# Sigmoid attention and a silu layer: the last two batches' first product by Strassen, after all attention

## The chip, the cores and the metric

The kernel runs on one core of a Trainium2 chip, as one launch. The metric is the device time of the launch in microseconds; the profile is of one execution, and its times are counted from that execution's first instruction. The engines are TensorE (PE, matrix products into PSUM), VectorE (DVE), ScalarE (ACT, activations and copies), GpSimd (POOL) and SyncE (SP, here only an issuer of transfers). Each engine works through its own queue in order; semaphores tie the queues together.

## The reference

```
q, k, v: 8 batches x 12 heads x 448 x 64 (float32);  w_in: 768 x 2048;  w_out: 2048 x 768
scores = q @ k.T / 8 - log(448)
x      = sigmoid(scores) @ v            # heads joined: 3584 rows x 768
h      = x @ w_in                       # 3584 x 2048
g      = h * sigmoid(h)                 # silu
out    = g @ w_out                      # 3584 x 768
```

## The kernel before, in words

All operands are float16 on the chip. **Attention.** Heads are taken in 24 groups of four (three groups a batch, two pairs each), and the 448 keys of a group in 7 chunks of 64, `NCH`; one (group, chunk) is a *tile*. `scores` (line 182) makes a tile with four 64x64 matmuls of 448 columns into PSUM `psc`, and ACT turns it into `attnT` by a sigmoid. `values` (line 218) multiplies the seven tiles of a group by v in 28 matmuls into `pav`, and DVE writes the result, times 64 (`SX`), to `xT[b]`, two of its six slices of 128 rows by 448. A batch is *ready* when its three groups are done. k and q are cast, put into rows (`kr`, `qr`) and transposed by transfers on SP's queue, four groups ahead (`dma_transpose`).

**h.** `h_unit(b, fc)` (line 255) makes one of 16 slices of 128 columns of h for batch b, transposed: six accumulating matmuls of 448 columns into `ph`. ACT takes the sigmoid (`tsig`) and DVE multiplies `ph` by it into `gTr`, which holds 16 slices for a pair of batches (896 columns).

**out.** `out_set` (line 319) makes 256 rows of the output by Strassen's scheme: seven products of 8 matmuls of 384 columns over blocks of `gTr` (sums `S1` to `S4` of them, made by DVE at the set's start) and of w_out (sums `T1` to `T4`, made once), with ACT copying the first product to `m1` and DVE adding up the rest (`plus`) into `osb`. Its first product reads slices 0 to 7 of the first block, its second slices 8 to 15. A pair of batches has 7 blocks of 128 rows: three sets, and the seventh blocks of two pairs (one of them put aside in `kept` by ACT) share a fourth.

**Order.** The kernel writes the order out itself; nothing is rescheduled. h and out are one generator, `all_moe` (line 421), that yields after each matmul. Attention runs in bursts of two or three tiles (`burst`, line 586), and after each burst `stretch` (line 449) pulls matmuls from the generator until a pace in nanoseconds is used up, with other weights for h (0.72) and for sets (1.28):

```
paces = {1: 1600, 2: 2400, 3: 2500, 4: 3400, 5: 3200, 6: 3000, 7: 2800}
        ns = paces[n // NT_B]
        tiles = burst(n, TILES[n // NT_B])
        n += tiles
        stretch(ns * tiles / 2)
```

What is left of the generator when attention ends runs alone. In the last pair that is: h of batch 6, its first set while batch 7's attention still runs, then h of batch 7, two sets and the shared set. PSUM is split into two double banks (`pssc`, for scores) and four single ones (`ps1`, for everything else), SBUF into tagged pools that are reused in turn.

Of the kernel before, what the change touches and what calls it, by code (L numbers as in the profile page):

```python
# [17 lines left out]
def kernel(  # L18
# [9 lines left out]
    nc = tc.nc  # L28
# [116 lines left out]
    def pe_transpose(g, pieces=(("k", 0, 4), ("k", 4, NCH), ("q", 0, 4), ("q", 4, NCH))):  # L145
        if ("k", g) not in qkT:
            new_qkT(g)
        for name, c0, c1, *copy in pieces:
# [12 lines left out]
                dst[:, c0 * P : c1 * P], ptr[:, : (c1 - c0) * P]  # L161
            )

    def dma_transpose(g, name, copy):
        if ("k", g) not in qkT:
            new_qkT(g)
        rows = p3.tile([P, NCH, 2, D], F16, tag=f"{name}r", name=f"{name}r")
        copy(rows, flat[name, g].rearrange("p j c d -> p c j d"))  # L168
        nc.sync.dma_start_transpose(
            out=qkT[name, g], in_=rows.rearrange("p c j d -> p (c j d)")  # L170
        )

    attnT = {}

    late = []

# [5 lines left out]
    def scores(g, ch, banks=None, put_off=False):  # L182


        attnT[g, ch] = p12.tile([P, 2, S], F16, tag="attnT", name="attnT")
        if banks is None:
            psc = ps_sc.tile([P, 2, 512], F32, tag="pssc", name="psc")
            banks = [psc[:, j] for j in range(2)]
            parts = [(attnT[g, ch], psc[:, :, :S])]
        else:  # L190
            parts = [(attnT[g, ch][:, j], banks[j][:, :S]) for j in range(2)]
        for half in range(2):
            own = slice(half * HP, (half + 1) * HP)
            for j in range(2):
                rows = slice(j * D, (j + 1) * D)
                nc.tensor.matmul(  # L196
                    banks[j][own, :S],
                    qkT["k", g][rows, ch, own],
                    qkT["q", g][rows, :, own],
                    start=True,  # L200
                    stop=True,
                )
        if put_off:
            late.extend(parts)
            return
        for to, psc in parts:
            nc.scalar.activation(to, psc, AF.Sigmoid, bias=bias_s, scale=QKSCALE)  # L207
# [10 lines left out]
    def values(g, end=NCH):  # L218
        b, iq = divmod(g, NQ)
        if b not in xT:  # L220
            assert b < 2 or b - 2 in h_done
            xT[b] = p2.tile([P, NPAIR, S], F16, tag="xT", name="xT")
        pav, done_rounds = part_of.pop(g, None) or (
            [ps_1.tile([P, 512], F32, tag="ps1", name="pav") for _ in range(2)],
            0,
        )
        for ch in range(done_rounds, end):
            at = attnT.pop((g, ch))
            for half in range(2):
                own = slice(half * HP, (half + 1) * HP)  # L230
                for j in range(2):
                    nc.tensor.matmul(  # L232
                        pav[half][j * D : (j + 1) * D, :S],
                        flat["v", g][own, j, ch, :],
                        at[own, j, :],
                        start=(ch == 0),
                        stop=(ch == NCH - 1),
                    )
        if end < NCH:
            part_of[g] = pav, end  # L240
            return
        for half in range(2):
            nc.vector.tensor_scalar_mul(xT[b][:, half * NQ + iq, :], pav[half][:, :S], SX)  # L243
        if iq == NQ - 1:
            ready.add(b)

# [69 lines left out]
    def row_blocks(m, g):  # L316
        return [rows_of[2 * m + u // NCH, u % NCH] for u in (2 * g, 2 * g + 1)]

    def out_set(a1, rows1, a2, rows2, last=False):
        nonlocal hold, weight  # L320
        weight = SET_WEIGHT
        lo, hi = slice(0, NHC), slice(NHC, NFC)
        osb = [p4.tile([P, DMODEL], F32, tag="osb", name="osb") for _ in range(2)]
        c11, c12 = (osb[0][:, nh * NO2 : (nh + 1) * NO2] for nh in range(2))
        c21, c22 = (osb[1][:, nh * NO2 : (nh + 1) * NO2] for nh in range(2))
        m1 = p2.tile([P, NO2], F32, tag="m1", name="m1")
        sg = [cpool.tile([P, NHC, P], F16, tag=f"S{i}", name=f"S{i}") for i in range(1, 5)]

        def store(rows, o, cols, engines):
            for at, (row, eng) in enumerate(zip(rows, engines)):  # L330
                eng.dma_start(row[:, cols], o[at * HP : (at + 1) * HP, cols])

        left, right, whole = slice(0, NO2), slice(NO2, DMODEL), slice(0, DMODEL)

        def product(a, w):
            po = ps_1.tile([P, 512], F32, tag="ps1", name="po")
            for fc in range(NHC):
                nc.tensor.matmul(  # L338
                    po[:, :NO2], a[:, fc, :], w[:, fc, :], start=(fc == 0), stop=(fc == NHC - 1)
                )  # L340
                if fc < NHC - 1:
                    yield 163
            return po[:, :NO2]

        def plus(o, po, x, sign=ISX):
            nc.vector.scalar_tensor_tensor(  # L346
                out=o, in0=po, scalar=sign, in1=x, op0=ALU.mult, op1=ALU.add
            )

        nc.vector.tensor_sub(sg[2], a1[:, lo], a2[:, lo])  # L350
        nc.vector.tensor_add(sg[0], a2[:, lo], a2[:, hi])
        po = yield from product(a1[:, lo], wq[0][0])
        nc.scalar.activation(m1, po, AF.Copy, scale=ISX)  # L353
        late_sigmoid()
        nc.vector.tensor_sub(sg[1], sg[0], a1[:, lo])
        hold = False
        yield 163
        po = yield from product(a1[:, hi], wq[1][0])
        plus(c11, po, m1)
        nc.vector.tensor_sub(sg[3], a1[:, hi], sg[1])  # L360
        if last:
            store(rows1, osb[0], left, (nc.sync, nc.sync))
        yield 163
        po = yield from product(sg[2], tw[3])
        plus(c22, po, m1)
        yield 163
        po = yield from product(sg[1], tw[2])
        plus(c22, po, c22)
        plus(c12, po, m1)
        yield 163  # L370
        po = yield from product(a2[:, hi], tw[4])
        plus(c21, po, c22, -ISX)
        yield 163
        po = yield from product(sg[0], tw[1])
        plus(c22, po, c22)
        plus(c12, po, c12)
        store(rows2, osb[1], whole, (nc.sync, nc.sync))
        yield 163
        po = yield from product(sg[3], wq[1][1])
        plus(c12, po, c12)  # L380
        if last:
            store(rows1, osb[0], right, (nc.sync, nc.scalar))
        else:
            store(rows1, osb[0], whole, (nc.sync, nc.sync))
        yield 163


    by_h1 = {3: 6, 6: 7, 9: 8}
    early = [h_unit(0, fc) for fc in range(2)]
    sums = w_sums()  # L390

    def moe_h(b):
        for fc in range(NFC):
            yield from early[fc] if b == 0 and fc < 2 else h_unit(b, fc)
            if b == 1:
                if fc >= 2:
                    next(sums)
                if fc in by_h1:
                    for name in ("k", "q"):
                        dma_transpose(by_h1[fc], name, act_copy)  # L400
                    if by_h1[fc] == 8:

                        nc.gpsimd.tensor_copy(gate, qkT["q", 8][:1, 0, :1])
                        for to in (10, 11, 12):
                            load("kq", to)

    def moe_set(m, g):
        step = out_set(block(g), row_blocks(m, g), block(g + 1), row_blocks(m, g + 1))
        for i, ns in enumerate(step):
            if m % 2 == 0 and g == 2 and i % 8 == 4 and i < 32:  # L410
                fcs = slice(i // 8 * 4, i // 8 * 4 + 4)
                nc.scalar.activation(kept[:, fcs], block(NCH - 1)[:, fcs], AF.Copy)
            if m == 0 and g == 0 and i in (10, 14):
                next(sums)
            if m == 0 and g == 0 and i in (24, 40):
                dma_transpose(9, "k" if i == 24 else "q", nc.vector.tensor_copy)
                if i == 40:
                    load("kq", 13)
            yield ns

    def all_moe():
        for m in range(B // 2):
            yield from moe_h(2 * m)
            if m > 0:
                yield from moe_set(m, 0)
            yield from moe_h(2 * m + 1)
            if m == 0:
                yield from moe_set(m, 0)
            yield from moe_set(m, 2)
            yield from moe_set(m, 4)  # L430
            if m % 2 == 1:
                g = NCH - 1
                yield from out_set(
                    kept, row_blocks(m - 1, g), block(g), row_blocks(m, g), m == B // 2 - 1
                )

    later = []
# [144 lines left out]
            do(*what)  # L582

    TILES = {2: 3, 3: 2, 4: 3, 5: 3, 6: 3, 7: 3}
    paces = {1: 1600, 2: 2400, 3: 2500, 4: 3400, 5: 3200, 6: 3000, 7: 2800}
    def burst(n, tiles):

        new = units[n : n + (tiles if not waiting else 2)]
# [56 lines left out]
```

## Time and profile before

| | |
|---|---|
| median of 3 runs | 378.19 us (377.76 to 378.33) |
| the profiled execution | 377.84 us, span 376.0 us |
| granted TensorE clock | 1.000 |
| busy: PE, DVE, ACT, POOL | 367.9, 233.9, 243.2, 66.1 us |
| h matmuls (128x448) | 768 |
| output matmuls (128x384) | 784 |

A line of a group reads: line of the kernel, engine, operation, what is written and from what, shapes, count, then busy microseconds and mean nanoseconds of one, then the idle time of that engine just before them and who ended it. Busy PE is modelled from pipelined matmuls, so the spacing of matmuls in the chain of waits is the better price of one: the last 96 of h and the last 168 of out stand there as one piece each. Start to start, operations of one engine come closer than their means say, since the end of one overlaps the next.

### The profile page before, as it was taken

How to read it: one execution, taken by the hardware profiler on the slowest of the kernel's cores; microseconds unless marked ns; L12 is line 12 of the kernel's file. 1: busy time of each engine (PE TensorE's matmuls, PEld its weight loads, DVE VectorE, ACT ScalarE, POOL GpSimd, SP SyncE). 2: the span in 40 equal slices, each digit the busy share in tenths (PEclk: the TensorE clock that was granted, in tenths of full speed). 3: DMA queues.
4: the chain of work that ended last, by engine and by line, in shares of the span. 5: the costliest groups of instructions: out<-in, count | busy, mean ns of one | idle time of the engine just before them, and what ended most of it. 6: DMA issues, size and time to landing. Idle time of an engine off the chain costs nothing.

```text
span 376.0 us, 7623 instructions
## 1 busy us (share of the span) xinstructions
PE 367.9 (98%) x3081; PEld 189.2 (50%) x3081; DVE 233.9 (62%) x417; ACT 243.2 (65%) x355; POOL 66.1 (18%) x99
## 2 busy tenths in 40 slices
PE   7999999999999999999999999999999999999995
PEld 3554445555554455455555545544555445555663
DVE  2664447997666466548676547645675457556773
ACT  5998886778766866676557676677866685243000
POOL 8566432053211002102120200000010000000000
PEclk9999999999999999999999999999999999999999
DMA  8999999959999909909499834546072300200333
GB/s 131 200 204 201 205 203 204 180 89 142 215 178 182 217 2 111 189 32 118 71 160 161 145 92 75 51 108 75 0 149 36 85 2 2 54 30 2 83 86 84
DMA packets 65698, 42.79 MB, mean 114 GB/s; under 512 B 36096, under 2 KB 62208, under 8 KB 65664
## 3 DMA queue, kind: packets, MB, share of 16 engines
q0 software_dynamic: 27072, 22.58, 42.5%
q1 hardware_dynamic: 38240, 19.44, 29.0%
q8 instruction: 24, 0.39, 0.4%
q10 hardware_dynamic: 352, 0.30, 0.2%
q14 instruction: 10, 0.08, 0.1%
HBM read 45.61 MB, written 11.01 MB: 151 GB/s over the span
## 4 chain that ended last, share of the span: by engine, by line
PE 91%; DMA 3%; ACT 2%; POOL 2%; issue 1%; DVE 0%; POOLq 0%; ACTq 0%
PE ph L262 38%; PE po L338 34%; PE psc L196 9%; PE pav L232 8%; DMA qf<-in_q_dram 3%; ACT attnT L207 1%; POOL kf L82 1%; POOL vf L82 1%; PE ptrq L153 0%; POOL qf L82 0%; ACT tsig L274 0%; DVE gTr L276 0%; ACT attnT L180 0%; PE ptrk L153 0%; DVE osb L346 0%
## 5 line engine op out<-in xcount | busy, mean ns | idle before, releaser
L207 ACT ACTIVATE attnT<-psc,bias_s 128x896 f16<-128x896 f32 (+1 forms) x168 | 138.5, 894 | 45.1 <-PE psc L196 44.9
L262 PE MATMUL ph<-xT,w_in_sb 128*128 128x448 f16 x768 | 151.2, 353 | 0.0
L276 DVE TENSOR_TENSOR gTr<-ph,tsig 128x448 f16<-128x448 f32 x128 | 78.3, 623 | 71.4 <-ACT tsig L274 70.9
L262 PEld LDWEIGHTS <-w_in_sb 128*128 128x128 f16 x768 | 72.8, 98 | 74.0 <-issue 9.2
L274 ACT ACTIVATE tsig<-ph 128x448 f16<-128x448 f32 x128 | 68.3, 549 | 49.1 <-PE ph L262 48.2
L338 PEld LDWEIGHTS <-S 128*128 128x128 f16 x448 | 42.3, 98 | 33.5 <-issue 7.2
L346 DVE SCALAR_TENSOR_TENSOR osb<-po,osb 128x384 f32<-128x384 f32 x70 | 37.6, 554 | 22.2 <-PE po L338 21.9
L196 PE MATMUL psc<-qT,kT 64*64 64x448 f16 x672 | 49.1, 360 | 1.5 <-ACT qT L143 0.5
L243 DVE TENSOR_SCALAR xT<-pav 128x448 f16<-128x448 f32 x48 | 27.7, 620 | 28.9 <-PE pav L232 28.9
L82 POOL DMA_DIRECT2D vf<-in_v_dram x24 | 17.2, 718 | 161.0 <-PE pav L232 138.6
L338 PE MATMUL po<-T,S 128*128 128x384 f16 x224 | 40.6, 327 | 0.0
L338 PEld LDWEIGHTS <-gTr 128*128 128x128 f16 x304 | 28.7, 98 | 23.5 <-issue 5.4
L338 PE MATMUL po<-w_out_sb,S 128*128 128x384 f16 x224 | 39.9, 326 | 0.0
L232 PE MATMUL pav<-attnT,vf 64*64 64x448 f16 x672 | 38.1, 350 | 0.4 <-DVE gTr L276 0.4
L338 PE MATMUL po<-w_out_sb,gTr 128*128 128x384 f16 x192 | 34.9, 327 | 0.0
L196 PEld LDWEIGHTS <-kT 64*64 64x64 f16 x672 | 16.4, 105 | 28.3 <-issue 23.1
L232 PEld LDWEIGHTS <-vf 64*64 64x64 f16 x672 | 20.9, 107 | 12.6 <-issue 2.7
L346 DVE SCALAR_TENSOR_TENSOR osb<-po,m 128x384 f32<-128x384 f32 x42 | 23.2, 553 | 6.3 <-PE po L338 5.1
L180 ACT ACTIVATE attnT<-psc,bias_s 128x896 f16<-128x896 f32 x26 | 26.6, 1022 | 0.0
L353 ACT ACTIVATE m<-po 128x384 f32<-128x384 f32 x14 | 6.9, 495 | 23.7 <-PE po L338 23.7
L338 PE MATMUL po<-T,gTr 128*128 128x384 f16 x112 | 21.4, 326 | 0.0
L82 POOL DMA_DIRECT2D kf<-in_k_dram x25 | 18.0, 721 | 18.0 <-DVE kr L168 9.6
(43 smaller groups left out, 153.6 us busy)
## 6 DMA issues: line engine op xcount, KB each, us to landing
out_dram<-osb SPq DMA_DIRECT2D x54, 192.0 KB, 3.2
vf<-in_v_dram POOLq DMA_DIRECT2D x24, 224.0 KB, 6.1
kf<-in_k_dram POOLq DMA_DIRECT2D x23, 224.0 KB, 7.9
qf<-in_q_dram POOLq DMA_DIRECT2D x23, 224.0 KB, 8.1
w_in_sb<-in_moe_w_in_dram POOLq DMA_DIRECT2D x16, 192.0 KB, 8.3
w_out_sb<-in_moe_w_out_dram POOLq DMA_DIRECT2D x4, 768.0 KB, 15.7
kT<-kr SPq DMA_TRANSPOSE x18, 7.3
qT<-qr SPq DMA_TRANSPOSE x18, 6.7
```

What stands on the lines that cost most here:

```text
L82: nc.gpsimd.dma_start(flat[name, g][:, :, c0:c1].rearrange("p i c d -> p i (c d)"), rows_in(name, g)[:, :, c0 * D : c1 * D],)
L180: nc.scalar.activation(to, psc, AF.Sigmoid, bias=bias_s, scale=QKSCALE)
L196: nc.tensor.matmul(banks[j][own, :S], qkT["k", g][rows, ch, own], qkT["q", g][rows, :, own], start=True, stop=True,)
L207: nc.scalar.activation(to, psc, AF.Sigmoid, bias=bias_s, scale=QKSCALE)
L232: nc.tensor.matmul(pav[half][j * D : (j + 1) * D, :S], flat["v", g][own, j, ch, :], at[own, j, :], start=(ch == 0), stop=(ch == NCH - 1),)
L243: nc.vector.tensor_scalar_mul(xT[b][:, half * NQ + iq, :], pav[half][:, :S], SX)
L262: nc.tensor.matmul(ph[:, :S], w_in_sb[:, cc, fc * P : (fc + 1) * P], xT[b][:, cc, :], start=(at == 0), stop=(at == NCC - 1),)
L274: nc.scalar.activation(tsig, ph[:, :S], AF.Sigmoid, bias=0.0, scale=ISX)
L276: nc.vector.tensor_mul(gTr[:, fc, (b % 2) * S : (b % 2) * S + S], ph[:, :S], tsig)
L338: nc.tensor.matmul(po[:, :NO2], a[:, fc, :], w[:, fc, :], start=(fc == 0), stop=(fc == NHC - 1))
L346: nc.vector.scalar_tensor_tensor(out=o, in0=po, scalar=sign, in1=x, op0=ALU.mult, op1=ALU.add)
L353: nc.scalar.activation(m1, po, AF.Copy, scale=ISX)
```

## The change

For the pair of batches 6 and 7, `h_pair` takes the place of the 32 `h_unit`s. x of the two batches is read as a 2 x 2 matrix of blocks (the lower and upper three slices of `xT`, even and odd batch), w_in as another (the lower and upper half of its columns and rows), and h as a third (slices f and 8 + f of the two batches). In eight rounds, one for each f, seven products of three matmuls replace eight. The first product is copied by ACT to a float32 tile (`mid`, m1); "six" and "seven" are added to it in turn by DVE (u2, u3), "five" makes u4 and c22, "two" makes c11, and "three" and "four" complete u4 and c21: in even rounds DVE adds "three", in odd rounds ACT copies it and GpSimd adds, and "four" is always copied by ACT and added by GpSimd. Silu is one activation from these tiles into `gTr`; that of c22 comes at once, the others are put off until behind the next round's copy of m1. The first two rounds have their first and second products ahead of all others.

Sums of w_in (`w_in_sum`, 16 operations of DVE, into buffers that q and k no longer need) are made in h of batch 5 and the sets of pair 2; sums of x (`x_sums`, 4 for each of three groups) right after the last batch's `values`. All attention ends ahead of the first round, by shorter paces from batch 4 on. The sets of pair 3 all follow `h_pair`; pair 2 has its sets behind both of its h. Since silu takes out the factor 64, `out_set` has its scale as an argument, and `kept` is rescaled when copied.

```diff
@@ values
+        if b == B - 1:
+            x_sums(iq)
...
+    w_in_sums = [(i, t) for t in range(4) for i in (3, 1, 2, 4)]
...
+    def x_sums(iq):
+        even, odd = xT[B - 2], xT[B - 1]
...
+        b11, b12, b21, b22 = even[:, iq], odd[:, iq], even[:, NH + iq], odd[:, NH + iq]
+        nc.vector.tensor_sub(xs[1, iq], b12, b11)
+        nc.vector.tensor_sub(b12, b22, b12)
+        nc.vector.tensor_sub(xs[2, iq], b22, xs[1, iq])
+        nc.vector.tensor_sub(xs[4, iq], b21, xs[2, iq])
+        xs[3, iq] = b12
+
+    def h_pair():
...
+        def product(o, f, a, x):
+            for c in range(NH):
+                nc.tensor.matmul(o, a(f, c), x(c), start=(c == 0), stop=(c == NH - 1))
+                if c < NH - 1:
+                    yield 189
...
+        def silu(fc, b, h):
+            nc.scalar.activation(
+                gTr[:, fc, b % 2 * S : (b % 2 + 1) * S], h, AF.Silu, bias=0.0, scale=ISX
+            )
...
+        def first(f):
+            assert even in ready and not w_in_sums
+            one, m1 = single(), middle()
+            yield from product(one, f, quadrant(0, 0), x_part(0, even))
+            act_copy(m1, one)
+            while put_off:
+                silu(*put_off.pop(0))
+            yield 189
+            return m1
+
+        def second(f, two, m1, c11):
+            yield from product(two, f, quadrant(0, 1), x_part(1, even))
+            nc.vector.tensor_add(c11, two, m1)
+            put_off.append((f, even, c11))
+            yield 189
+
+        def group(f, m1):
+            assert odd in ready
+            u2, u3, u4, c22, c21 = (middle() for _ in range(5))
+            six, seven = pair()
+            yield from product(six, f, w_sum(2), x_sum(2))
+            nc.vector.tensor_add(u2, six, m1)
+            yield 189
+            yield from product(seven, f, w_sum(3), x_sum(3))
+            nc.vector.tensor_add(u3, seven, u2)
+            yield 189
+            five, two = pair()
+            yield from product(five, f, w_sum(1), x_sum(1))
+            nc.vector.tensor_add(u4, five, u2)
+            nc.vector.tensor_add(c22, five, u3)
+            silu(NHC + f, odd, c22)
+            yield 189
+            if f > 1:
+                yield from second(f, two, m1, m1)
+            three, four = single(), single()
+            yield from product(three, f, w_sum(4), x_part(1, odd))
+            if f % 2 == 0:
+                nc.vector.tensor_add(u4, three, u4)
+            else:
+                act_copy(u2, three)
+                nc.gpsimd.tensor_add(u4, u2, u4)
+            put_off.append((f, odd, u4))
+            yield 189
+            yield from product(four, f, quadrant(1, 1), x_sum(4))
+            act_copy(c21, four)
+            nc.gpsimd.tensor_add(c21, c21, u3)
+            put_off.append((NHC + f, even, c21))
+            yield 189
+
+        m1s = []
+        for f in range(2):
+            m1s.append((yield from first(f)))
+        for f in range(2):
+            yield from second(f, single(), m1s[f], middle())
+        for f in range(NHC):
+            m1 = m1s[f] if f < 2 else (yield from first(f))
+            yield from group(f, m1)
+        while put_off:
+            silu(*put_off.pop(0))
+        h_done.update((even, odd))
...
     def all_moe():
         for m in range(B // 2):
-            yield from moe_h(2 * m)
-            if m > 0:
-                yield from moe_set(m, 0)
-            yield from moe_h(2 * m + 1)
-            if m == 0:
+            if m == B // 2 - 1:
+                yield from h_pair()
+            else:
+                yield from moe_h(2 * m)
+                if m == 1:
+                    yield from moe_set(m, 0)
+                yield from moe_h(2 * m + 1)
+            if m != 1:
                 yield from moe_set(m, 0)
             yield from moe_set(m, 2)
             yield from moe_set(m, 4)
...
-    paces = {1: 1600, 2: 2400, 3: 2500, 4: 3400, 5: 3200, 6: 3000, 7: 2800}
+    paces = {1: 1600, 2: 2400, 3: 2500, 4: 2800, 5: 2500, 6: 2350, 7: 2300}
```

## The prediction

> **What bounds the kernel now.** I read the engine table first, then the end of the chain of waits, then the groups of instructions, and last the busy time by stretches.
>
> ```profile
> PE 367.9 (98%) x3081; PEld 189.2 (50%) x3081; DVE 233.9 (62%) x417; ACT 243.2 (65%) x355; POOL 66.1 (18%) x99
> 326.42 18.16 PE ph L262 x96
> 344.58 27.31 PE po L338 x168
> 371.92 0.56 DVE osb L346
> ```
>
> TensorE (PE) sets the time; VectorE (DVE) and ScalarE (ACT) have room. The next two lines give its prices: an h matmul takes 18.16/96 = 0.1892 us, an output matmul 27.31/168 = 0.1626. Attention ends at 323.5; from there the chain is PE alone until 371.9, and the tail after that is the same in both kernels.
>
> ```profile
> L276 DVE TENSOR_TENSOR gTr<-ph,tsig 128x448 f16<-128x448 f32 x128 | 78.3, 623 | 71.4 <-ACT tsig L274 70.9
> L274 ACT ACTIVATE tsig<-ph 128x448 f16<-128x448 f32 x128 | 68.3, 549 | 49.1 <-PE ph L262 48.2 <-DVE T L308 0.6
> L353 ACT ACTIVATE m<-po 128x384 f32<-128x384 f32 x14 | 6.9, 495 | 23.7 <-PE po L338 23.7
> L481 ACT ACT_TABLE_LOAD x1 | 1.3, 1283 | 1.3 <-PEq L629 1.3
> L143 ACT ACTIVATE qf<-qs 128x384 f16<-128x384 f32 x1 | 0.5, 522 | 1.5 <-DMA qs<-in_q_dram 1.5
> masks.py:199 POOL TENSOR_SCALAR_AFFINE_SELECT ident<-ident 128x128 f16<-128x128 f16 x1 | 0.3, 289 | 0.1
> masks.py:197 POOL MEMSET ident<- 128x128 f16 x1 | 0.2, 224 | 0.0
> L629 POOL MEMSET const-float32-1.0<- 128x1 f32 x1 | 0.1, 93 | 0.0
> 75.00:112.00 37.00, 36.99 (x345) 19.33 (x344) 28.28 (x53) 27.72 (x39) 11.67 (x17) 1.00 1.13 155
> ```
>
> These price the new small operations, by mean ns. The last line (busy PE, PEld, DVE, ACT, POOL) is the one that vouches for denser attention: PE was full for 37 us there.
>
> **What is removed.** h of batches 6 and 7 takes 192 matmuls; seven products of 3 in each of 8 rounds are 168. 24 x 0.1892 = **-4.54 us** of PE. 32 sigmoids (17.6 us) and 32 multiplications (19.9 us) go too, off the path.
>
> **What is moved.** From batch 4 on attention runs in denser bursts, so that its last value product ends 31 output and 12 h matmuls (5.04 + 2.27 us) ahead of the first group of products. In pair 2's output sets a cycle of 8 tiles now has 44 output matmuls: PE 44 x 0.1626 + 32 score matmuls at 0.058 + 28 value matmuls at 0.047 = 10.3 us. ACT takes, start to start, 2.8 us for three tiles (1.92 + 0.89 in the timeline at 298 and 300 us) and 1.8 for two (88.8 to 90.6), so 7.4 a cycle, plus 0.4 for m. From 75 to 112 us bursts stand 17, 17 and 12 output matmuls apart, nearly the same density, and PE lost nothing but some 0.24 us in one burst. In h of batch 5, 69 matmuls lie in a cycle (16.3 us of PE; ACT 7.4 + 11.5 sigmoids x 0.45 = 12.6). I take +0.3 for the denser part; bounds -0.3 (a stall of the old schedule goes) to +1.2.
>
> **What DVE gets.** 16 sums of w_in (128x768 f16, 0.55 us by the sums of w_out) and 12 of x (128x448, about 0.38 by the same slope). They hide beside PE work in which DVE still has room: a cycle of h of batch 5 gives it 11.5 multiplications and 2 evictions (0.53 each, start to start), as many sums (0.47) and 2 copies (0.53), 13.6 of 16.3 us; the last x sums are done some 3 us after the last value product, against the 7.3 us above. Nothing for them; with the cover gone it would be those 3 us less what PE still had. Loads into w_in, kf and kr tiles are over by then, no DMA is added, and SP's transposes only come earlier.
>
> **The new part: a chain between ACT and DVE.** PE needs 21 x 0.1892 = 3.97 us a round. Prices: a copy from PSUM 0.55 (next start 0.45 later); silu from SBUF 0.575 (the 522 of 384 elements plus 64 x 0.83; next start 0.48 later); a DVE add 0.62, next start 0.53, or 0.65 where it needs the one before; 0.03 to another engine; a PE product of three 0.57, seen 0.20 after its slot. GpSimd's add of 128x448 f32 has no row: by the memsets 1.02 ns an element, by the affine select 1.5, and both streams with the 0.09 of a small one give 1.2 us. I take 1.2; bounds 0.78 (affine select's slope alone) and 2.0 (that slope for each input, the memset's for the output).
>
> Call s the start of the copy m1. u2 starts s+0.58, u3 s+1.23, u4 s+1.76, c22 s+2.29 and ends s+2.91. ACT has done its three put-off silus by s+1.9 and waits: silu of c22 at s+2.94. Then, in its queue, the copy of "three" (odd rounds only), the copy of "four", and only then the next round's m1. So m1 follows m1 after 3.87 us in even rounds and **4.32 in odd ones**: 0.35 over PE's 3.97.
>
> Now from the first product of the pair at 0. The twelve first matmuls end at 2.27. c22 of round 0 ends 5.37; the table load (silu after sigmoid) holds ACT to 6.68; round 1's c22 ends 8.21, and m1 of round 2 starts 9.62, where PE had it ready at 8.71. Six silus stand put off there instead of three: m1 of round 3 at 13.88, then 18.21, 22.08, 26.41, 30.28. PE alone would allow 28.56. PE itself isn't held: its nearest release (c11 of round 6 at 29.9, for "two" of round 7) comes 0.2 early, so it ends at 31.8.
>
> But the first output set reads all that ACT still owes. c22 of round 7 ends 33.20, silu 33.23, copies 33.71 and 34.16, silu of c11 34.61 to 35.18. Product 1's eighth matmul wants it at 32.9: a wait of 2.3. GpSimd's u4 is done at 35.5 and c21 at 36.7, its silu at 37.3; product 2's eighth matmul then waits another 0.8. **+3.1 us**; bounds +2.3 (GpSimd 0.78) and +4.9 (1.6); silu at 0.65 would make +4.2.
>
> The row of the table load is 1.28 us, and the one activation behind it started at once, at 2.56. The Trainium skill, ScalarE: Activation LUTs, "What ACT_TABLE_LOAD costs", adds a drain of about 1.38 us to every switch; the trace shows none, but nothing ran ahead of that load, so it can't settle it (a rival below).
>
> The Trainium skill's GPSIMD Engine Reference, section 3.1, gives 4497 ns for such an add of 2048 elements, twice DVE's; by that slope ours is an estimated 1.0 us and the wait would be 2.7 instead of 3.1.
>
> **Sum.** -4.54 + 0.3 + 3.1 = -1.1 us. The profiled execution took 377.84 (span 376.0 and 1.84 around it), 0.35 under the median 378.19. So 376.7 by the profiled one, **377.1** as a median.
>
> **Rivals.**
> *The chain keeps up (0.15).* If odd rounds take no more than 3.97 us, only the end's own latency is left: "three" is seen 0.37 us before PE ends, copied 0.58 later, two GpSimd adds and a silu follow, 3.2 us after PE's end, against 15 output matmuls (2.44): 0.8. Then -4.5 + 0.3 + 0.8 = -3.4: 374.8. For it: 0.35 us over four ACT steps and four adds is little. Against: each price is a row's.
> *The switch drains (0.12).* 1.38 us more at round 0; the even rounds and PE's slack take back half, and the wait at the set becomes 3.8: -0.4, 377.8. By the Trainium skill's page above this is what happens.
> *GpSimd binds, slower (0.16).* In an odd round its first add starts s+4.00. With 2.0 us an add, c21 is ready at s+8.0, and its silu stands in ACT's queue ahead of the next c22: two rounds take 9.4 instead of 8.2. Three such pairs and 1.6 at the end add 5.4: wait 8.5, so +4.3, 382.4. It decides from 1.5 us an add (there 4.2, the gain gone). For it: no two-input GpSimd row; against: 1.2 by the rows.
> *Denser bursts stall (0.07), also slower.* If each of the 20 three-tile bursts from batch 4 on loses the 0.24 us seen once at 99.8, +4.8 in place of 0.3: +3.4, 381.6. Against: that row is single.
> *Not what it says:* excluded; the instruction order shows 168 products and the last attention ahead of the first group.
>
> **How the numbers follow.** Forecast 0.50. About 0.2%, 0.76 us, is what a measurement of this kernel tells from no change. The forecast's own range (waits of 2.3 to 4.9, the 0.3 at its bounds) is 375.7 to 379.8, three quarters of it faster: 0.37, with 0.10 same and 0.03 slower. The chain that keeps up adds 0.15 faster; the drain 0.04, 0.06, 0.02; GpSimd and bursts 0.23 slower. Faster 0.56, same 0.16, slower 0.28. Range 374.7 to 380.2: it takes in the forecast's own range, the drain, and the near parts of the others (a chain half kept up, GpSimd at 1.6).
>
> **What would show it.** Right: h matmuls 744, PE full up to the first output set; there a gap of about 3 us, ended by ACT's silu; idle ACT on DVE's c22 in each round; m1 starts 3.9 and 4.3 apart; GpSimd adds near 1.2. Wrong: GpSimd over 1.5, idle PE within the rounds, score matmuls waiting for sigmoids before the pair, or a gap at the set under 1 us.

## The result, and the profile after

The changed kernel is slower: a median of 395.29 us (394.03 to 395.99, 5 runs) against 378.33 us (377.76 to 378.66, 5 runs), a ratio of 1.0446 (95% interval 1.0421 to 1.047). The forecast was 377.1 and the range 374.7 to 380.2. The profiled execution took 395.99 us with a span of 394.0 us, 18.0 more than before.

From the page of the changed kernel, the engine table and two rows of the span in 40 slices (busy tenths of PE, and its granted clock); then the end of its chain of waits (start, length, what; most pieces of 0.04 us left out):

```profile
PE 368.9 (94%) x3057; PEld 188.1 (48%) x3057; DVE 250.8 (64%) x457; ACT 253.4 (64%) x376; POOL 79.9 (20%) x111
PE   7899999999999999999999999999999766679995
PEclk9999999999999999999999999999999999899999
```

```profile
301.83 0.58 PE ph L483 x3
...
326.23 0.64 DVE mid L533
326.91 0.74 PE ph L483 x3
327.73 0.62 DVE mid L536
328.36 0.53 DVE mid L540
328.89 0.54 DVE mid L541
329.47 1.88 PE ph L483 x9
331.43 0.55 ACT mid L143
...
355.01 0.58 ACT gTr L501
355.64 34.15 PE po L346 x209
389.81 0.56 DVE osb L354
```

The 24 matmuls are gone (3057 in place of 3081), and PE is full up to slice 30, counted from 0. The loss lies in slices 31 to 35, which are the pair. The second block is most of one round of it: u2 (L533), then "seven" on PE, u3, u4 and c22 (L536, L540, L541), then "two", "three" and "four" on PE, then a copy on ACT, and so on. The chain goes through PE twice a round, each time behind DVE. The prediction has neither wait: by the arithmetic, "seven" needs nothing from u2 and "two" nothing from c22. The list of PE's waits in the changed kernel says the same (who waited for whom, then us in total, times, longest):

```profile
PE ph L483 <- DVE mid L541: 7.6, 6, 1.3
PE ph L483 <- DVE mid L533: 7.0, 8, 1.5
```

Eight times, once a round, PE waited for the DVE operation of line 533, which makes u2; six times, in rounds 2 to 7, for that of line 541, which makes c22.

The 17.0 us between the two kernels, from the first h matmul of batch 1 (at 56.50 and 57.40 us) to the last addition, come apart as follows: -4.5 for the matmuls, +18.4 in the rounds (the pair takes 50.2 us, from 301.83 to the first output matmul at 352.0, where its 168 matmuls need 31.8; some 1.7 of the 18.4 is a dip of the clock, see the last section), +1.2 at the first output set, and about +1.9 ahead of the pair, in attention and the sums (1.1 and 0.6 of it in the profiles of the two kernels below that separate them). The last 0.9 us of the span are a later start, which differs from run to run.

### The profile page after: what moved, and what is told of

Same layout as the page of the kernel before. It is cut to its first block, busy times and chain, and to the rows that moved or that the text cites. A ratio compares the mean times of both kernels' runs of the same rounds, so it can differ in the third digit from the quotient of the medians.

```text
span 394.0 us, 7685 instructions
## 1 busy us (share of the span) xinstructions
PE 368.9 (94%) x3057; PEld 188.1 (48%) x3057; DVE 250.8 (64%) x457; ACT 253.4 (64%) x376; POOL 79.9 (20%) x111
## 4 chain that ended last, share of the span: by engine, by line
PE 81%; DVE 6%; ACT 4%; DMA 3%; POOL 2%; issue 2%; POOLq 1%; DVEq 0%; ACTq 0%
PE po L346 31%; PE ph L270 27%; PE psc L202 9%; PE pav L238 8%; PE ph L483 6%; DMA kf<-in_k_dram 3%; ACT attnT L213 2%; ACT mid L143 2%; DVE mid L533 1%; DVE mid L536 1%; DVE mid L541 1%; DVE mid L540 1%; POOL kf L82 1%; POOL vf L82 1%; POOLq L851 1%
## 5 line engine op out<-in xcount | busy, mean ns | idle before, releaser
L270 PE MATMUL ph<-xT,w_in_sb 128*128 128x448 f16 x576 | 114.4, 353 | 0.0
L284 DVE TENSOR_TENSOR gTr<-ph,tsig 128x448 f16<-128x448 f32 x96 | 58.4, 621 | 51.7 <-ACT tsig L282 51.1
L270 PEld LDWEIGHTS <-w_in_sb 128*128 128x128 f16 x576 | 54.1, 98 | 56.5 <-issue 9.0
L282 ACT ACTIVATE tsig<-ph 128x448 f16<-128x448 f32 x96 | 50.8, 552 | 24.6 <-PE ph L270 24.2
L501 ACT ACTIVATE gTr<-mid 128x448 f16<-128x448 f32 x32 | 16.8, 573 | 12.3 <-DVE mid L541 10.9
```

The lines of the kernel that those rows point to most:

```text
L270: nc.tensor.matmul(ph[:, :S], w_in_sb[:, cc, fc * P : (fc + 1) * P], xT[b][:, cc, :], start=(at == 0), stop=(at == NCC - 1),)
L282: nc.scalar.activation(tsig, ph[:, :S], AF.Sigmoid, bias=0.0, scale=ISX)
L284: nc.vector.tensor_mul(gTr[:, fc, (b % 2) * S : (b % 2) * S + S], ph[:, :S], tsig)
```

## The experiments

*Theory A:* two products that share a two-bank PSUM tile (`pair()` gives six and seven the two banks of one tile, five and two those of another) are kept apart by the semaphores as if they were one buffer. A matmul that starts the second bank waits until DVE has read the first. *Rival B:* the chain of copies, additions and silus of the prediction is by itself as long as the measured 6.3 us a round. *Rival C:* the denser attention costs much of it.

### own_tiles: no two products in one tile

```diff
-            six, seven = pair()
+            six, seven = double(), single()
...
-            five, two = pair()
+            five, two = double(), single() if f > 1 else None
```

`double()` is one bank of a two-bank tile whose other bank stays empty. Products, additions and their order are those of the changed kernel.

> The changed kernel with one edit: six and five get a double-bank tile each of which only one bank is used, seven and two get single banks, so no two products share a tile. Theory A (in the changed kernel the first matmul of seven waits for DVE's u2, which reads six out of the same two-bank tile, and two waits for c22, which reads five): these waits go, the pair takes 32 to 35 us instead of 50, no dip of the clock, and the kernel comes to 377 to 381 us. Rival B (the chain ACT copy, DVE adds, silu, copies is by itself as long as the measured 6.3 us a round): the rounds stay near 6 us and the time over 390 us.

Measured: 379.77 us, 1.0041 of before (1.0026 to 1.0056), 15.5 us below the changed kernel. Its waits of PE on the pair's products, all of them:

```profile
PE ph L483 <- DVE mid L523: 0.5, 2, 0.3
```

(L523 makes c11; "seven" takes over the bank that c11 of the round before reads.) Theory A holds and B falls: 14.6 us of waits on u2 and c22 are gone with nothing changed but the tiles. What is left of the chain can now be read. These are its silus of c22, which ACT waits for, in rounds 3 to 7 (start, length, engine and line, count, then idle time before and who ended it):

```profile
318.34 0.58 ACT L501 ACTIVATE gTr<-mid 128x448 f16<-128x448 f32 x1 [1.04 <-DVE mid L540]
322.73 0.58 ACT L501 ACTIVATE gTr<-mid 128x448 f16<-128x448 f32 x1 [0.46 <-DVE mid L540]
326.74 0.58 ACT L501 ACTIVATE gTr<-mid 128x448 f16<-128x448 f32 x1 [1.17 <-DVE mid L540]
331.13 0.58 ACT L501 ACTIVATE gTr<-mid 128x448 f16<-128x448 f32 x1 [0.45 <-DVE mid L540]
335.14 0.58 ACT L501 ACTIVATE gTr<-mid 128x448 f16<-128x448 f32 x1 [1.17 <-DVE mid L540]
```

They stand 4.39, 4.01, 4.39 and 4.01 us apart, alternating as foretold (4.32 and 3.87). The first output set still waits for them:

```profile
334.52 1.30 PE L346 MATMUL po<-w_out_sb,gTr 128*128 128x384 f16 x7
337.11 1.47 PE L346 MATMUL po<-w_out_sb,gTr 128*128 128x384 f16 x8 [1.29 <-ACT gTr L501]
339.56 0.34 PE L346 MATMUL po<-w_out_sb,gTr 128*128 128x384 f16 x1 [0.98 <-ACT gTr L501]
```

By starts, the eighth matmul is 1.45 us late (334.52 plus 7 of 0.163 is 335.66) and the sixteenth 1.15: 2.6 us where the prediction had 3.1.

### plain_pair: the moved attention alone

```diff
-                yield from h_pair()
+                yield from moe_h(B - 2)
+                yield from moe_h(B - 1)
```

The paces and the order of the changed kernel; no sums of w_in or x; one scale for all sets, as before.

> The changed kernel's paces and order (all attention ahead of the pair, the sets of the last pair behind it) with h of batches 6 and 7 made by plain units (192 matmuls, sigmoid and multiplication) and no sums of w_in or x. It measures the moved attention alone. Theory A (nearly all of the loss is inside the pair): 378 to 381 us, at most 1 per cent above the kernel before. Rival C (the denser attention costs much of it): over 384 us.

Measured: 379.44 us, 1.0029 of before (1.0016 to 1.0042). Rival C falls too: the moved attention costs 1.2 us of the 17.0. In the chain of waits twelve score matmuls take 0.69 us and eight take 0.50 where nothing holds them. These bursts are longer:

```profile
183.82 0.30 PE psc L202
184.13 0.76 PE psc L202 x11
248.73 1.00 PE psc L202 x12
286.70 0.66 PE psc L202 x8
```

The first two lines are one burst, of 1.07 us with the 0.01 between them. So the three lose 0.38, 0.31 and 0.16 us, and two more (at 226.33 and 283.23) lose 0.10 and 0.07. The trace names no wait behind these. At pair 2's first set a score matmul waits for ACT, but the kernel before pauses at the same place:

```profile
271.04 0.38 PE psc L196 x4
```

Eight score matmuls there take 0.77 us to the next instruction's start, and 0.65 in the kernel before. All together that is 1.1 us, the difference of the two profiles.

### share_six_seven and share_five_two: one shared tile at a time

```diff
 share_six_seven, against own_tiles
-            six, seven = double(), single()
+            six, seven = both()
 share_five_two, against own_tiles
-            five, two = double(), single() if f > 1 else None
+            five, two = both()
```

Here `both()` gives the two banks of one tile, as `pair()` did.

> own_tiles with one shared tile given back: six and seven are the two banks of one tile, five and two keep tiles of their own. It prices the wait of seven for u2 alone. The changed kernel's waits before seven were about 0.8 us in 8 rounds and, behind a late m1, make the round longer: 5 to 8 us above own_tiles if the waits simply add; if either wait alone already locks PE to the chain of ACT and DVE, near the full 15 us above own_tiles.

> own_tiles with the other shared tile given back: five and two are the two banks of one tile, six and seven keep tiles of their own. It prices the wait of two for c22 alone: 6 rounds of about 1.3 us in the changed kernel, so 6 to 9 us above own_tiles if waits add; near 15 us if one of them alone locks PE to the chain.

Measured: 386.08 us (1.0203 of before, 1.0189 to 1.0217) and 387.66 us (1.0247, 1.0233 to 1.0261). Against own_tiles that is 6.3 and 7.9 us, 14.2 together of the 15.5 (by the ratios 6.1 and 7.8, since the kernel before itself took 0.2 us more beside these two). Each brings back just its own wait, first of share_six_seven, then of share_five_two:

```profile
PE ph L483 <- DVE mid L535: 7.4, 8, 1.5
```

```profile
PE ph L483 <- DVE mid L543: 9.8, 6, 2.4
```

(L535 is u2 and L543 is c22 there.) The waits add: each puts a part of DVE's chain in line with PE, and neither alone locks PE to the whole. The 1.3 us missing to 15.5 may be the clock's dip in the changed kernel (some 1.7 us in its profile, last section): its one run at clock 1.0 took 394.03 us, 14.3 above own_tiles. That is one run, so it is not shown.

### put_off_c22: the silu of c22 put off as well

```diff
-            silu(NHC + f, odd, c22)
+            put_off.append((NHC + f, odd, c22))
```

Against own_tiles: all four silus of a round follow the next round's copy m1.

> As own_tiles, and the silu of c22 is put off with the other three, so that ACT has no wait for the chain of adds between its copies. The prediction's chain (odd rounds 4.3 us, a drain at the first set) says that own_tiles still loses 1 to 3 us there and that this one is 0.5 to 1.5 us faster than own_tiles, PE full through the rounds. If ACT's order does not matter once the tiles are apart, the two are equal within 0.4 us.

Measured: 377.45 us, 0.9979 of before (0.9966 to 0.9991), 2.3 us below own_tiles, more than expected. The prediction's chain is confirmed by taking it away: in own_tiles ACT's silus had waited 4.8 us for c22 (and 2.3 for GpSimd's additions); with the wait for c22 went the alternation of rounds, and PE's last 84 matmuls of the pair follow in one piece of 16.12 us. What stayed is a single jam in rounds 2 and 3, behind eight silus in a row, and 0.5 us at the set:

```profile
310.25 1.28 ACT L501 ACT_TABLE_LOAD   x1
311.55 3.84 ACT L501 ACTIVATE gTr<-mid 128x448 f16<-128x448 f32 x8
315.30 0.94 ACT L143 ACTIVATE mid<-ph 128x448 f32<-128x448 f32 x2
```

### drained and drained_paces: both edges

```diff
 drained, against put_off_c22
         for f in range(2):
             yield from second(f, single(), m1s[f], middle())
+        while put_off:
+            silu(*put_off.pop(0))
...
-            if f % 2 == 0:
+            if f % 2 == 0 or f == NHC - 1:
                 nc.vector.tensor_add(u4, three, u4)
...
+            if f == 1 or f == NHC - 1:
+                while put_off and (f > 1 or len(put_off) > 2):
+                    silu(*put_off.pop(0))
             yield from product(four, f, quadrant(1, 1), x_sum(4))
-            act_copy(c21, four)
-            nc.gpsimd.tensor_add(c21, c21, u3)
+            if f == NHC - 1:
+                nc.vector.tensor_add(c21, four, u3)
+            else:
+                act_copy(c21, four)
+                nc.gpsimd.tensor_add(c21, c21, u3)
 drained_paces, against drained
-    paces = {1: 1600, 2: 2400, 3: 2500, 4: 2800, 5: 2500, 6: 2350, 7: 2300}
+    paces = {1: 1600, 2: 2400, 3: 2500, 4: 2800, 5: 2500, 6: 2400, 7: 2450}
```

> put_off_c22 with the two edges drained: the first two silus (and the table load) ahead of the first group while ACT is idle, round 1 and the last round give out their silus before product four, and the last round's two additions are made by VectorE out of PSUM, without GpSimd. Theory (what put_off_c22 still loses is 0.9 us of PE in rounds 2 and 3, behind eight silus in a row, and 0.5 us at the first set): 1.0 to 1.5 us below put_off_c22, 376.0 to 376.5 us, 0.5 per cent below the kernel before. If those waits only move, equal to put_off_c22 within 0.4 us.

> drained with the last two batches' paces eased (6: 2400, 7: 2450 in place of 2350 and 2300), so that attention's last bursts stand 18 and 12 output matmuls apart and its end comes 23 instead of 31 output matmuls ahead of the pair. If the 1.2 us of plain_pair come from the density of the last bursts, 0.3 to 0.8 us below drained; if from the first set behind h of batch 5 alone, equal to it; if the sums of x now come too late for the first group, slower.

Measured: 375.90 us, 0.9933 of before (0.992 to 0.9945), and 375.18 us, 0.9917 (0.9904 to 0.9931). The end of drained's chain of waits:

```profile
300.97 11.36 PE ph L483 x60
312.34 0.62 DVE mid L535
313.00 20.02 PE ph L483 x105
333.02 36.41 PE po L346 x224
369.46 0.56 DVE osb L354
```

The 224 output matmuls now follow in one piece: no wait at the set, and one short stop in the rounds. Easing the last paces took another 0.7 us off the median, at the upper end of what was expected. The traces can't show where: the two profiled executions took the same (375.38 and 375.43 us), and the ranges of the two kernels overlap. The end product is a kernel 0.8% faster than before: of the 4.5 us of matmuls, 3.2 arrive.

## Why the prediction was wrong

**The step that failed** is "PE itself isn't held: its nearest release (c11 of round 6 at 29.9, for 'two' of round 7) comes 0.2 early". It took each bank as released by its own reader, so that "seven" waited for u3 of the round before and "two" for c11 of the round before, nearly a round away. In the run "seven" waited for u2 and "two" for c22 of the *same* round, which read the other bank of the same tile; own_tiles and the two share kernels show that the shared tile is the reason. With that, PE stands in line with the chain instead of beside it, and a round of the chain is u2 0.64, seven 0.74, u3 to c22 1.69, "two" to the next "one" 2.44, a copy of 0.55 and the hand-overs: some 6.3 us in place of 3.97. The code showed it (one tile, two products, a reader between them), but the prediction didn't quote `pair()` and didn't ask what else reads that tile. "Not what it says: excluded" was true of the order and beside the point: the order was as said, the waits were not.

**The chain itself was right.** Its prices met the rows: a silu 573 ns (0.575 foretold), a copy 542 (0.55), an addition 614 to 624 (0.62), GpSimd's addition 1.13 us (1.2, bounds 0.78 to 2.0), the table load 1283 ns. So did its form, as own_tiles shows: rounds of 4.39 and 4.01, 2.6 us at the set for 3.1. That PE loses nothing inside the rounds was a little off even there: from 301.65 to 334.52 the 168 matmuls took 32.9 us, 1.1 over their own 31.8, and PE waited twice, 0.26 us each, for the c11 that the prediction had 0.2 early.

**Attention** was under-sized: 1.2 us by plain_pair for 0.3 foretold, at the upper bound given. The stretch that vouched for it, 75 to 112 us, held two long bursts, not one: beside the 0.24 us at 99.8, eight score matmuls from 95.73 on took 0.71 us instead of 0.50. Its row (36.99 us busy of 37) hid both, since busy PE is modelled. Five more of 0.07 to 0.38 us came in the denser part. What holds them stays open. **The sums** were put at nothing and cost 0.6: own_tiles enters the pair 244.45 us after the first h matmul of batch 1 (301.65 less 57.20), plain_pair 243.81 (300.73 less 56.92). All of it is in one place: the last value product takes 2.09 us, start to next start, in own_tiles (294.35 to 296.44) and 1.45 in plain_pair (294.06 to 295.51). In own_tiles it stops after two matmuls until DVE, with x sums and set sums queued ahead, has read a bank. The 7.3 us of cover lie behind this product and couldn't help.

**The rivals.** GpSimd did not bind (1.13 us, under the 1.5 from which it would), and "denser bursts stall" happened, in a few bursts and at a quarter of its price. The drain behind the table load did not come: in put_off_c22 the load follows the copies without a break, and the silu behind it starts at 311.55, 1.30 us after the load began. The Trainium skill's ScalarE: Activation LUTs, "What ACT_TABLE_LOAD costs", has 1.38 us more there; this trace decides against it.

## What to carry to other kernels

Ask of every buffer what the *unit of waiting* is. Two results in one tile, with a reader of the first between the writers, turn a parallel pair into a chain, even where they lie in different banks; it cost 6 to 8 us a pair of products here, and a tile for each gave it back with no other change. A count of saved matmuls is worth its face value only where the engine that saves them never stands behind another: look, for each first matmul of a product, at which engine it waits for. And put off what an in-order engine would wait for: one silu a round, moved in ACT's queue, was worth 2.3 us.

## What the hardware showed that was not expected

**The clock dips in a stretch without a long gap.** In the changed kernel's profile TensorE's granted clock fell in the middle of the pair, for less than 5 us (columns: the stretch, its length, busy PE, PEld, DVE, ACT and POOL with their instructions, then the clock):

```profile
302.00:336.00 34.00, 23.54 (x118) 11.30 (x116) 19.05 (x33) 17.99 (x35) 7.84 (x7) 1.00 0.09 24
336.00:340.00 4.00, 4.00 (x13) 1.67 (x12) 0.62 (x1) 1.52 (x3) 1.13 (x1) 0.57 0.00 0
337.00:339.00 2.00, 2.00 (x6) 0.76 (x5) 0.62 (x1) 0.54 (x1) 0.18 (x1) 0.50 0.00 0
```

PE had been busy for 69% of the 34 us before, and its longest single wait there was 1.5 us. From 341 us on the clock was 1.00 again. At the lowest point three matmuls took 1.12 us from one start to the next, 0.37 each, twice the usual 0.189. In the chain the 15 matmuls from 335.87 on took 4.69 us, and 15 such matmuls at 309.13 took 3.01. The profiles of share_six_seven and share_five_two, in which PE is busy for 82% and 79% of the 50 us from 302 on, show no dip there (clock 1.00). What sets it off stays open. The five runs had mean clocks of 0.993 to 1.0, and the one at 1.0 was the fastest (394.03 us). The Trainium skill's TensorE: Matmul & The Clock Gate, Part 1, has a gate that gives either the full or half the clock by how busy PE was of late; the halving agrees.

**GpSimd's addition and DVE's sum held each other.** In own_tiles eleven of twelve additions on GpSimd take 1.13 to 1.15 us; the last takes 1.58, and in the changed kernel the same one does. Only there does GpSimd add beside a DVE operation with two inputs in SBUF, the set's first sum:

```profile
353.30 0.69 DVE L358 TENSOR_TENSOR S<-gTr 128x1024 f16<-128x1024 f16 x1 [1.61 <-ACT gTr L501]
353.39 1.58 POOL L557 TENSOR_TENSOR mid<-mid 128x448 f32<-128x448 f32 x1
```

In put_off_c22 GpSimd's last addition starts first. It keeps its 1.13 us, and DVE's sum takes 1.26 instead of 0.69:

```profile
334.96 1.13 POOL L556 TENSOR_TENSOR mid<-mid 128x448 f32<-128x448 f32 x1
335.39 1.26 DVE L358 TENSOR_TENSOR S<-gTr 128x1024 f16<-128x1024 f16 x1 [1.33 <-ACT gTr L501]
```

In drained, whose last round leaves GpSimd out, the same sum takes 0.68. The additions that DVE makes in the rounds read one input from PSUM and held nobody. The Trainium skill's SBUF — State Buffer, "SBUF: two separate sides", describes such a lock between the two engines for a DVE operation with two SBUF inputs, with the first to start going first; the 0.45 and the 0.57 us agree with it. So in these runs whichever starts second is held; that the two SBUF inputs are the reason is argued, since no run changed them alone.
